# Adding a unit's two key blocks into one square before the transpose, and splitting it by two masks after

## The chip, the core and the metric

The kernel runs on one core of one Trainium2 chip. The metric is the device time of one execution in microseconds (us); lower is better. The engines are named as the profile names them: PE (TensorE matmul) and PEld (its weight load), DVE (VectorE), ACT (ScalarE), POOL (GpSimd) and SP (SyncE, whose queue issues the DMAs).

## What is computed

Attention with four sink keys and a sliding window of 128, for 4 batches of 8 heads, 768 positions and 64 dimensions per head, followed by a feed-forward layer on the 3072 x 512 result:

```python
scores = scale * np.matmul(q, k.transpose(0, 1, 3, 2))
rel = pos[:, None] - pos[None, :]
keep = (pos[None, :] < n_sink) | ((rel >= 0) & (rel < window))
scores = np.where(keep, scores, -1000000000.0)
a = np.exp(scores - scores.max(-1, keepdims=True))
x = (a / (a.sum(-1, keepdims=True) + 1e-09)) @ v      # heads side by side: 3072 x 512
r = np.maximum(x @ w_in, 0.0)                         # 3072 x 2048
out = (s * (r * r) + b) @ w_out                       # 3072 x 512
```

Everything is float32. The kernel keeps that precision on PE by splitting each operand into a rounded high part and a remainder (hi and lo), and by adding two or three products of the parts.

## The kernel before

**Chunks and steps.** The 3072 rows are eight chunks of 384 (half a batch each). The feed-forward layer of chunk c runs while the attention of chunk c+1 is computed, in one interleaved program (lines 672 to 682). A chunk's feed-forward is 32 steps: for each of 16 blocks f of the inner dimension, l1(f) is 12 matmuls of 384 columns into `h` (L521), followed by L524 and L528 on ACT and L526 and L529 on DVE, which make `g`; l2(f), which stands two blocks later, is 9 matmuls of 512 columns into `po` (L540). Between the steps stand the slots of the next chunk's attention. The attention of chunk 0 has a form of its own (`first_slots`), and the feed-forward of chunk 0 carries, beside the attention of chunk 1, the preparation of the weights: per block f, ACT L198 and L199, DVE L200 and L201, POOL L203, ACT L208, and L214 on DVE or, for every fourth block, on POOL. The last chunk's feed-forward has no attention beside it.

**Units.** One attention unit is a head h and a block i of 128 queries; a chunk has 24 units, and unit t starts in slot t. `unit_a` makes the scores with two matmuls (L293, L294) into `sc`; DVE L298 adds the mask and takes the row minimum of the negated scores; ACT L304 takes the exponential into `sm`; POOL L305 copies the sink columns into `psk`. A unit's `sm` holds two key blocks of 128 columns, the block before the query block (at column p0) and the query block's own (at c0), and 16 sink columns. Since the window is 128, the mask leaves in the earlier block only keys above the diagonal and in the own block only keys on or below it: of a query's 256 entries, position j of one block or position j of the other is zero. Chunks of odd number start in the middle of a batch, and all 24 of their units have two blocks; in chunks of even number the 8 units with i = 0 have no earlier block (g = 0, p0 is None) and 16 have two.

**From exponentials to output.** `unit_b`, LB = 2 slots after `unit_a`, transposes both blocks on PE (L316 for the earlier block, L317 for the own one) into the PSUM tile `tp`; ACT L321 writes the rounded part of `tp` to `hl`, DVE L322 the remainder. `unit_c`, LC = 4 slots after `unit_a`, multiplies `hl` by the values (L354), copies with ACT L362 and adds with DVE L363 into `xm`, and at the end of a pair of heads transposes `psk` (L367) and makes `xsk` of it (ACT L369, DVE L370). `unit_d`, one slot later (LD), has two matmuls (L378, L380), DVE L381 and L382, ACT L383 and POOL L384, which write the pair's part of the next feed-forward's input. `prep_head` splits a head's queries (ACT L268, DVE L272), keys (ACT L271, POOL L273) and values (ACT L277, POOL L278); `load_sinks` has ACT L259 and POOL L260.

**What sets the order.** The program is written as the loops above; a list scheduler of the kernel language puts the instructions of each engine in order when the kernel is built, and each engine then works through its own list in that order. Tiles come from pools of buffers: a write into a buffer waits until the readers of what it held are done. `sm` has four buffers, `hl` two, `xm` two, and all tiles named by `ps` (`sc`, `tp`, `h`, `o`, `ts`, `os`, `zb`) share five banks of PSUM.

Of the kernel before, what the change touches and what calls it, by code (L numbers as in the profile page):

```python
# [6 lines left out]
F32 = mybir.dt.float32  # L7
# [5 lines left out]
ALU = mybir.AluOpType  # L13
AX = mybir.AxisListType

P = 128
# [3 lines left out]
CH = BLK * P  # L20
# [6 lines left out]
MDT = mybir.dt.bfloat16  # L27
# [6 lines left out]
E0, LB0, LC0 = 8, 4, 6  # L34
LB, LC, LD, L2 = 2, 4, 1, 2


@with_exitstack
def tile_kernel(ctx, tc, qT, kT, k0, v, vsk, n_sink, window, w, s, b, out):
    nc = tc.nc  # L40
    w, n_sink, window = (a.bitcast(I32) for a in (w, n_sink, window))
    const = ctx.enter_context(tc.tile_pool(name="const", bufs=1))
# [7 lines left out]
    wk = wk_cm.__enter__()  # L50
# [8 lines left out]
    ident = identr.bitcast(F32)  # L59
# [4 lines left out]
    W = 2 * P + NS  # L64
    msk = const.tile([P, 3 * W + P + NS], MDT, tag="msk", name="msk")
    m_1, m_odd, m_even = (msk[:, j * W:(j + 1) * W] for j in range(3))
    m_0 = msk[:, 3 * W:]
# [29 lines left out]
    def mask(out, keep):  # L97
        nc.vector.tensor_scalar(out=out, in0=keep, scalar1=BIG, scalar2=-BIG, op0=ALU.mult, op1=ALU.add)
# [31 lines left out]
    def constants2():  # L130
# [16 lines left out]
        mask(m_1[:, 2 * P:], tm2[:, :NS])  # L147
        mask(m_even[:, P:P + NS], snk[:, :NS])
        cp = nc.gpsimd.tensor_copy
        upm, lom = m_full[2][:, P:2 * P], m_full[2][:, 2 * P:]  # L150
# [130 lines left out]
    def unit_a(k, h, i):  # L281

        hd = k.heads[h]
# [5 lines left out]
        else:  # L289
# [13 lines left out]
        hh = h % 2  # L303
        nc.scalar.activation(sm[:, :n], sm[:, :n], AF.Exp, bias=negm[:, uu], scale=-1.0, accum_out=pp.zz[:, i, hh:hh + 1])  # L304
        nc.gpsimd.tensor_copy(out=pp.psk[:, i, :6 * NS].rearrange("p (t x) -> p t x", t=3)[:, :, hh * NS:(hh + 1) * NS],  # L305
                              in_=sm[:, s0:s0 + NS].unsqueeze(1).to_broadcast([P, 3, NS]))

    def unit_b(k, h, i):
# [5 lines left out]
        tp = ps("tp")  # L314
        if p0 is not None:
            nc.tensor.transpose(tp[:, :P], sm[:, p0:p0 + P], ident)  # L316
        nc.tensor.transpose(tp[:, P:2 * P], sm[:, c0:c0 + P], ident)  # L317

        a, z = (P if p0 is None else 0), 2 * P
        hi, lo = (hd.hl[:, t, i * z + a:(i + 1) * z] for t in range(2))  # L320
        nc.scalar.copy(hi, tp[:, a:z])  # L321
        nc.vector.tensor_tensor(out=lo, in0=tp[:, a:z], in1=hi.bitcast(F32), op=ALU.subtract)  # L322
        pp = k.pairs[h // 2]
# [9 lines left out]
    def unit_c(k, h, i):  # L333
# [23 lines left out]
        if i == BLK - 1:  # L357
            a, c = (0, D) if h % 2 == 0 else (D, 0)
            if h % 2 == 0:
                pp.x = wk.tile([P, CH], F32, tag="xm", name="xm")  # L360
                pp.y = wk.tile([P, CH], F32, tag="y", name="y", bufs=1)
# [385 lines left out]
```

## Time and profile before

| | us |
|---|---|
| median of 3 timed runs | 783.27 |
| lowest and highest of them | 783.14, 783.36 |
| span of the profiled execution, first to last instruction | 782.6 |
| PE busy in it | 735.8 |
| DVE busy | 510.5 |
| ACT busy | 494.6 |
| POOL busy | 263.8 |

For the profiled execution only its span is recorded, with no total of its own; the span is 0.67 us below the median of the timed runs, and that remainder is taken to lie around it. The page and the views of the trace name a group of instructions by line, engine and operation, then by output and inputs (out<-in), then by shapes and count; the number after the bar is the busy time of the group in us and the mean of one in ns, then the idle time of the engine in front of them and what ended it. A row of the timeline gives start and duration in us. A row of the stretches (windows) gives the stretch, its length, and for each engine the busy time and the count of instructions, then the granted PE clock as a share of full speed, the DMA share and GB/s.

### The profile page before, as it was taken

How to read it: one execution, taken by the hardware profiler on the slowest of the kernel's cores; microseconds unless marked ns; L12 is line 12 of the kernel's file. 1: busy time of each engine (PE TensorE's matmuls, PEld its weight loads, DVE VectorE, ACT ScalarE, POOL GpSimd, SP SyncE). 2: the span in 40 equal slices, each digit the busy share in tenths (PEclk: the TensorE clock that was granted, in tenths of full speed). 3: DMA queues.
4: the chain of work that ended last, by engine and by line, in shares of the span. 5: the costliest groups of instructions: out<-in, count | busy, mean ns of one | idle time of the engine just before them, and what ended most of it. 6: DMA issues, size and time to landing. Idle time of an engine off the chain costs nothing.

```text
span 782.6 us, 12152 instructions
## 1 busy us (share of the span) xinstructions
PE 735.8 (94%) x4036; PEld 656.8 (84%) x4036; DVE 510.5 (65%) x1251; ACT 494.6 (63%) x1231; POOL 263.8 (34%) x411
## 2 busy tenths in 40 slices
PE   6878887599999999999999999999999999999996
PEld 3657675489989999999989999899989999899985
DVE  5888899985676466665676466765676466663231
ACT  4896977766676576656676576656676576643222
POOL 3146567752333234332333234322333234210000
PEclk9998999989999999999999999999999999999999
DMA  8644304212111211112111211112111211001001
GB/s 275 267 148 176 111 14 160 85 34 75 43 44 53 85 46 52 49 43 76 43 43 54 85 46 52 50 43 76 43 44 55 83 46 54 27 1 41 1 1 44
DMA packets 28118, 54.21 MB, mean 69 GB/s; under 512 B 3600, under 2 KB 16528, under 8 KB 26128
## 3 DMA queue, kind: packets, MB, share of 16 engines
q1 hardware_dynamic: 28048, 53.36, 21.3%
q8 instruction: 34, 0.56, 0.3%
q14 instruction: 36, 0.29, 0.1%
HBM read 47.06 MB, written 6.29 MB: 68 GB/s over the span
## 4 chain that ended last, share of the span: by engine, by line
PE 77%; DVE 7%; ACT 6%; POOL 4%; issue 3%; DMA 1%; SPq 1%; ACTq 0%; POOLq 0%; DVEq 0%
PE h L521 31%; PE po L540 30%; PE o L354 5%; PE sc L294 2%; PE sc L293 2%; POOL w L203 2%; PE tp L317 2%; PE tp L316 2%; DVE w L201 1%; ACT w L199 1%; DVE wt L200 1%; PE o L480 1%; DMA sb<-in_s 1%; ACT sm L304 1%; ACT w L208 1%
## 5 line engine op out<-in xcount | busy, mean ns | idle before, releaser
L521 PE MATMUL h<-x,w 128*128 128x384 f32 x1536 | 300.9, 345 | 14.3 <-DVE r L526 8.1
L540 PE MATMUL po<-w,g 128*128 128x512 f32 x1152 | 298.5, 401 | 4.3 <-DVE g L529 3.2
L521 PEld LDWEIGHTS h<-x,w 128*128 128x128 f32 x1536 | 270.5, 190 | 22.0 <-issue 5.9
L540 PEld LDWEIGHTS po<-w,g 128*128 128x128 f32 x1152 | 209.7, 189 | 45.7 <-DVE g L529 5.0
L524 ACT ACTIVATE r<-h 128x384 f32<-128x384 f32 x128 | 62.7, 490 | 109.4 <-PE h L521 102.3
L298 DVE CUSTOM_DVE_ANT_0 sm<-sc,msk 128x272 f32<-128x272 f32 (+1 forms) x168 | 70.2, 418 | 82.0 <-PE sc L294 60.2
L529 DVE SCALAR_TENSOR_TENSOR g<-r,sb,g 128x384 fp32r<-128x384 f32 x128 | 86.6, 677 | 45.1 <-ACT g L528 43.0
L526 DVE SCALAR_TENSOR_TENSOR r<-h,sb,r 128x384 f32<-128x384 f32 x128 | 78.5, 614 | 54.3 <-ACT r L524 54.1
L305 POOL COPY psk<-sm 128x48 f32<-128x48 f32 x168 | 51.8, 309 | 168.2 <-ACT sm L304 167.3
L304 ACT ACTIVATE sm<-sm,negm 128x272 f32<-128x272 f32 (+1 forms) x168 | 85.3, 508 | 22.9 <-DVE negm L298 22.0
L528 ACT ACTIVATE g<-r,sb 128x384 fp32r<-128x384 f32 x128 | 78.8, 615 | 29.3 <-DVE r L526 29.1
L273 POOL TENSOR_TENSOR kl<-kraw,kh 128x544 fp32r<-128x544 f32 (+1 forms) x56 | 71.8, 1282 | 56.4 <-ACT kh L271 54.5
L321 ACT CAST hl<-tp 128x256 fp32r<-128x256 f32 (+1 forms) x168 | 59.0, 352 | 27.5 <-PE tp L317 27.1
L354 PE MATMUL o<-hl,vv 128*128 128x256 f32 (+1 forms) x400 | 71.6, 295 | 1.8 <-DVE hl L322 0.9
L322 DVE TENSOR_TENSOR hl<-tp,hl 128x256 fp32r<-128x256 f32 (+1 forms) x168 | 66.6, 398 | 7.9 <-ACT hl L321 6.0
L278 POOL TENSOR_TENSOR vv<-vraw,vv 128x256 fp32r<-128x256 f32 (+1 forms) x56 | 42.9, 766 | 60.8 <-ACT vv L277 58.7
L354 PEld LDWEIGHTS o<-hl,vv 128*128 128x128 f32 x400 | 55.0, 190 | 4.1 <-issue 1.3
L363 DVE TENSOR_TENSOR xm<-o,y 64x384 f32<-64x384 f32 x56 | 31.0, 553 | 31.5 <-ACT y L362 31.3
L294 PE MATMUL sc<-kl,qs 128*128 128x272 f32 (+1 forms) x168 | 48.8, 290 | 0.4 <-POOL kl L273 0.4
L293 PE MATMUL sc<-kh,qs 128*128 128x272 f32 (+1 forms) x168 | 47.8, 284 | 0.7 <-DVE qs L272 0.4
L272 DVE TENSOR_TENSOR qs<-qraw,qs 64x384 fp32r<-64x384 f32 x56 | 42.5, 758 | 6.3 <-ACT qs L268 4.6
L317 PE MATMUL tp<-identr,sm 128*128 128x128 f32 x168 | 46.0, 274 | 0.0
(113 smaller groups left out, 838.7 us busy)
## 6 DMA issues: line engine op xcount, KB each, us to landing
w<-in_w SPq DMA_DIRECT2D x15, 1024.0 KB, 10.3
kraw<-in_kT SPq DMA_DIRECT2D x32, 272.0 KB, 2.6
out<-ot SPq DMA_DIRECT2D x24, 256.0 KB, 2.0
qraw<-in_qT SPq DMA_DIRECT2D x28, 192.0 KB, 2.4
kraw<-in_kT SPq DMA_DIRECT2D x24, 208.0 KB, 2.4
vraw<-in_v SPq DMA_DIRECT2D x16, 256.0 KB, 2.6
vraw<-in_v SPq DMA_DIRECT2D x12, 192.0 KB, 2.3
vsraw<-in_vsk SPq DMA_DIRECT2D x28, 64.0 KB, 1.8
```

The lines of the kernel that those rows point to most:

```text
L273: nc.gpsimd.tensor_tensor(out=hd.kl[:, :kw], in0=hd.k[:, :kw], in1=hd.kh[:, :kw].bitcast(F32), op=ALU.subtract)
L293: nc.tensor.matmul(sc[:, :n], hd.qs[:, qs], hd.kh[:, c0:c0 + n], start=True, stop=False)
L294: nc.tensor.matmul(sc[:, :n], hd.qs[:, qs], hd.kl[:, c0:c0 + n], start=False, stop=True)
L298: nc.vector.tensor_tensor_reduce(out=sm[:, :n], in0=sc[:, :n], in1=m, scale=-0.125, scalar=BIG, op0=ALU.add, op1=ALU.min, accum_out=negm[: ...
L304: nc.scalar.activation(sm[:, :n], sm[:, :n], AF.Exp, bias=negm[:, uu], scale=-1.0, accum_out=pp.zz[:, i, hh:hh + 1])
L322: nc.vector.tensor_tensor(out=lo, in0=tp[:, a:z], in1=hi.bitcast(F32), op=ALU.subtract)
L354: nc.tensor.matmul(hd.o[:, q0:q0 + n * P], hd.vv[:, kb, :], hd.hl[:, t, c0 * P:(c0 + n) * P], start=(hd.n == 0), stop=(i == BLK - 1 and kb ...
L521: nc.tensor.matmul(h[:, :CH], weight[f][:, 0, wi, cc * P:(cc + 1) * P], x[xi][:, cc, :], start=(i == 0), stop=(i == 11))
L526: nc.vector.scalar_tensor_tensor(out=r, in0=h[:, :CH], scalar=sw_ap, in1=r, op0=ALU.mult, op1=ALU.mult)
L528: nc.scalar.activation(gg[:, 0, :], r, AF.Identity, bias=b_ap, scale=1.0)
L529: nc.vector.scalar_tensor_tensor(out=gg[:, 1, :], in0=r, scalar=b_ap, in1=gg[:, 0, :].bitcast(F32), op0=ALU.add, op1=ALU.subtract)
L540: nc.tensor.matmul(po[tb], gg[:, gi, tsl], weight[f][:, 1, wi, :], start=(f == 0 and i == 0), stop=(f == NF - 1 and i == 2))
```

## The change

Units with two key blocks (144 of the 168 that `unit_a` and `unit_b` work on) get another path. Behind the exponential, POOL adds the earlier block of `sm` onto the own block (after.py L311, 128 x 128, both inputs and the output in SBUF), ahead of the copy of the sinks. `unit_b` transposes this one square (L322). DVE multiplies the transposed square, read twice from PSUM, by `split`, two masks of ones and zeros held as bf16, into a new SBUF tile `two` with one buffer (L332); ACT rounds `two` into `hl` (L334), and POOL instead of DVE takes the remainder (L335). The 24 units without an earlier block keep their one transpose, ACT copy and DVE remainder. Two small DVE instructions make `split`, once. `unit_b` comes three slots after `unit_a` (LB) instead of two and `unit_c` five (LC) instead of four, so that the distance from `unit_b` to `unit_c` stays at two slots; `xm` has one buffer instead of two.

```diff
--- before.py
+++ after.py
@@ -32,7 +32,7 @@
 NARROW, NEARLY = 2, 8
 RB, VB = 2, 2
 E0, LB0, LC0 = 8, 4, 6
-LB, LC, LD, L2 = 2, 4, 1, 2
+LB, LC, LD, L2 = 3, 5, 1, 2
 
 
 @with_exitstack
@@ -63,6 +63,7 @@
     n_ap, w_ap = nw[:, 0:1], nw[:, 1:2]
     W = 2 * P + NS
     msk = const.tile([P, 3 * W + P + NS], MDT, tag="msk", name="msk")
+    split = const.tile([P, 2, P], MDT, tag="split", name="split")
     m_1, m_odd, m_even = (msk[:, j * W:(j + 1) * W] for j in range(3))
     m_0 = msk[:, 3 * W:]
 
@@ -146,6 +147,8 @@
         mask(m_0[:, :NS], tmp[:, :NS])
         mask(m_1[:, 2 * P:], tm2[:, :NS])
         mask(m_even[:, P:P + NS], snk[:, :NS])
+        nc.vector.tensor_scalar(out=split[:, 0, :], in0=rel, scalar1=0.0, scalar2=None, op0=ALU.is_gt)
+        nc.vector.tensor_scalar(out=split[:, 1, :], in0=rel, scalar1=0.0, scalar2=None, op0=ALU.is_le)
         cp = nc.gpsimd.tensor_copy
         upm, lom = m_full[2][:, P:2 * P], m_full[2][:, 2 * P:]
         cp(out=m_0[:, NS:], in_=lom)
@@ -302,6 +305,10 @@
         s0 = k.cc[(h, i)][3]
         hh = h % 2
         nc.scalar.activation(sm[:, :n], sm[:, :n], AF.Exp, bias=negm[:, uu], scale=-1.0, accum_out=pp.zz[:, i, hh:hh + 1])
+        if g > 0:
+            c1 = k.cc[(h, i)][1]
+            p1 = k.cc[(h, i)][2]
+            nc.gpsimd.tensor_tensor(out=sm[:, c1:c1 + P], in0=sm[:, p1:p1 + P], in1=sm[:, c1:c1 + P], op=ALU.add)
         nc.gpsimd.tensor_copy(out=pp.psk[:, i, :6 * NS].rearrange("p (t x) -> p t x", t=3)[:, :, hh * NS:(hh + 1) * NS],
                               in_=sm[:, s0:s0 + NS].unsqueeze(1).to_broadcast([P, 3, NS]))
 
@@ -312,14 +319,20 @@
         if i == 0:
             hd.hl = wk.tile([P, 2, 2 * CH], F32R, name="hl", tag="hl", bufs=HLB)
         tp = ps("tp")
-        if p0 is not None:
-            nc.tensor.transpose(tp[:, :P], sm[:, p0:p0 + P], ident)
-        nc.tensor.transpose(tp[:, P:2 * P], sm[:, c0:c0 + P], ident)
-
-        a, z = (P if p0 is None else 0), 2 * P
-        hi, lo = (hd.hl[:, t, i * z + a:(i + 1) * z] for t in range(2))
-        nc.scalar.copy(hi, tp[:, a:z])
-        nc.vector.tensor_tensor(out=lo, in0=tp[:, a:z], in1=hi.bitcast(F32), op=ALU.subtract)
+        nc.tensor.transpose(tp[:, :P], sm[:, c0:c0 + P], ident)
+
+        z = 2 * P
+        if p0 is None:
+            hi, lo = (hd.hl[:, t, i * z + P:(i + 1) * z] for t in range(2))
+            nc.scalar.copy(hi, tp[:, :P])
+            nc.vector.tensor_tensor(out=lo, in0=tp[:, :P], in1=hi.bitcast(F32), op=ALU.subtract)
+        else:
+            hi, lo = (hd.hl[:, t, i * z:(i + 1) * z] for t in range(2))
+            two = wk.tile([P, 2, P], F32, tag="two", name="two", bufs=1)
+            nc.vector.tensor_tensor(out=two, in0=tp[:, :P].unsqueeze(1).to_broadcast([P, 2, P]), in1=split, op=ALU.mult)
+            flat = two.rearrange("p s c -> p (s c)")
+            nc.scalar.copy(hi, flat)
+            nc.gpsimd.tensor_tensor(out=lo, in0=flat, in1=hi.bitcast(F32), op=ALU.subtract)
         pp = k.pairs[h // 2]
         if h % 2 == 1 and i == BLK - 1:
             zr = wk.tile([P, 2, BLK, 2], F32, tag="zr", name="zr")
@@ -357,7 +370,7 @@
         if i == BLK - 1:
             a, c = (0, D) if h % 2 == 0 else (D, 0)
             if h % 2 == 0:
-                pp.x = wk.tile([P, CH], F32, tag="xm", name="xm")
+                pp.x = wk.tile([P, CH], F32, tag="xm", name="xm", bufs=1)
                 pp.y = wk.tile([P, CH], F32, tag="y", name="y", bufs=1)
             nc.scalar.copy(pp.y[a:a + D], hd.o[c:c + D, :CH])
             nc.vector.tensor_tensor(out=pp.x[a:a + D], in0=hd.o[a:a + D, :CH], in1=pp.y[a:a + D], op=ALU.add)
```

PE, in the middle of the attention of a chunk with an odd number: before, from the scores of one unit to the last product of the next, with one l2 step (`po`) between them.

```order
L293 MATMUL sc<-kh,qs 128x272
L294 MATMUL sc<-kl,qs 128x272
L316 MATMUL tp<-identr,sm 128x128
L317 MATMUL tp<-identr,sm 128x128
L354 MATMUL o<-hl,vv 128x256 x2
L354 MATMUL o<-hl,vv 128x128 x2
L540 MATMUL po<-w_792,g 128x512 x9
L293 MATMUL sc<-kh,qs 128x272
L294 MATMUL sc<-kl,qs 128x272
L316 MATMUL tp<-identr,sm 128x128
L317 MATMUL tp<-identr,sm 128x128
L354 MATMUL o<-hl,vv 128x128 x2
```

A place of the same kind in the changed kernel, two l2 steps further on (L296 and L297 are the scores, L322 the transpose, L367 the products with the values, L553 the l2 step).

```order
L296 MATMUL sc<-kh,qs 128x272
L297 MATMUL sc<-kl,qs 128x272
L322 MATMUL tp<-identr,sm 128x128
L367 MATMUL o<-hl,vv 128x256 x2
L367 MATMUL o<-hl,vv 128x128 x2
L553 MATMUL po<-w_971,g 128x512 x9
L296 MATMUL sc<-kh,qs 128x272
L297 MATMUL sc<-kl,qs 128x272
L322 MATMUL tp<-identr,sm 128x128
L367 MATMUL o<-hl,vv 128x128 x2
L367 MATMUL o<-hl,vv 128x256 x2
```

Each unit has one transpose fewer on PE; the scores, the products and the feed-forward steps stand as they stood.

POOL, in the feed-forward of chunk 0 while the weights are made: before, a stretch with two of the weight steps (L203); `vv` and `kl` are the splits of values and keys, `psk` the copy of the sinks.

```order
L278 TENSOR_TENSOR vv<-vraw,vv 128x4x64
L305 COPY psk_96<-sm 128x3x16
L305 COPY psk_95<-sm 128x3x16
L203 TENSOR_TENSOR w_801<-w_801 128x1024
L273 TENSOR_TENSOR kl<-kraw,kh 128x544
L305 COPY psk_95<-sm 128x3x16
L203 TENSOR_TENSOR w_896<-w_896 128x1024
```

The changed kernel, from one weight step (L206) to the next (`sm` is the new addition, `hl` the new remainder).

```order
L206 TENSOR_TENSOR w_802<-w_802 128x1024
L281 TENSOR_TENSOR vv<-vraw,vv 128x4x64
L311 TENSOR_TENSOR sm<-sm 128x128
L312 COPY psk_96<-sm 128x3x16
L335 TENSOR_TENSOR hl<-two,hl 128x256
L311 TENSOR_TENSOR sm<-sm 128x128
L312 COPY psk_96<-sm 128x3x16
L335 TENSOR_TENSOR hl<-two,hl 128x256
L311 TENSOR_TENSOR sm<-sm 128x128
L312 COPY psk_96<-sm 128x3x16
L335 TENSOR_TENSOR hl<-two,hl 128x256
L206 TENSOR_TENSOR w_900<-w_900 128x1024
```

Where one or two copies of sinks stood between two weight steps, three additions, three copies and three remainders now stand between these two.

## The prediction

> **What bounds the kernel now.** First the page: its engine line, and two rows of the span in 40 slices.
>
> ```profile
> PE 735.8 (94%) x4036; PEld 656.8 (84%) x4036; DVE 510.5 (65%) x1251; ACT 494.6 (63%) x1231; POOL 263.8 (34%) x411
> ...
> PE   6878887599999999999999999999999999999996
> DVE  5888899985676466665676466765676466663231
> ```
>
> PE is at 9 in every slice but the first eight and the last, and there DVE is the fuller engine. So one answer does not hold for the whole span, and I cut it into stretches: the feed-forward of chunk 0 with the making of the weights, a short run-out of it, the six chunks after it, and the last feed-forward alone.
>
> ```profile
> 56.00:164.00 108.00, 84.90 (x409) 68.96 (x408) 99.11 (x164) 82.75 (x167) 69.95 (x62) 0.92 0.31 106
> 164.00:182.50 18.50, 17.12 (x96) 15.15 (x96) 11.91 (x26) 10.81 (x26) 9.47 (x12) 1.00 0.23 74
> 182.50:708.00 525.50, 523.06 (x3013) 482.34 (x3012) 338.43 (x890) 339.47 (x899) 167.36 (x308) 1.00 0.18 51
> 708.00:782.60 74.60, 67.42 (x338) 60.55 (x336) 19.94 (x33) 20.15 (x37) 0.63 (x1) 0.98 0.06 23
> ```
>
> In the six chunks PE is busy 523.06 of 525.50 us (99.5%) at the full granted clock, with DVE and ACT at 64 to 65% and POOL at 32%. In the first stretch no engine is full: DVE 92%, PE 79%, ACT 77%, POOL 65%. The views of the waits say how they hold each other there, and that PE in the six chunks hardly waits at all (its only row):
>
> ```profile
> PE os L378 <- DVE xsk L370: 2.4, 6, 0.5
> ...
> ACT w L208 <- POOL w L203: 14.2, 10, 2.1
> PE h L521 <- DVE r L526: 8.1, 4, 5.5
> ```
>
> So in the six chunks the end is set by what PE has to do, and in the first stretch by a ring of DVE, ACT and POOL.
>
> **What goes from PE.** The changed part has one transpose where L316 and L317 stood. A busy time doesn't price it, since matmuls overlap; the starts do. One unit, with nothing but an l2 step behind it:
>
> ```profile
> 307.38 0.29 PE L293 MATMUL sc<-kh,qs 128*128 128x272 f32 x1
> 307.50 0.29 PE L294 MATMUL sc<-kl,qs 128*128 128x272 f32 x1
> 307.63 0.27 PE L316 MATMUL tp<-identr,sm 128*128 128x128 f32 x1
> 307.74 0.27 PE L317 MATMUL tp<-identr,sm 128*128 128x128 f32 x1
> 307.77 2.35 PE L540 MATMUL po<-w,g 128*128 128x512 f32 x9
> ```
>
> Four matmuls take 0.39 us of the stream (0.10 each), and L317 starts 0.11 after L316, L316 0.13 after L294. The chain of waits over the six chunks gives the same for all of them, with the count of L316 in that stretch in the second row:
>
> ```profile
> by line: PE h L521 38.3%; PE po L540 36.1%; PE o L354 6.7%; PE sc L294 3.1%; PE sc L293 3.0%; PE tp L317 2.7%; PE tp L316 2.3%; PE ts L367 1.1%; PE os L378 1.1%; PE zb L380 0.8%; ACT g L528 0.7%; DVE xsk L370 0.6%; DVE xm L363 0.6%; issue 0
> ...
> 182.50:708.00 525.50, 32.90 (x120) 16.74 (x120) 1.00 0.18 51
> ```
>
> L316 is 2.3% of 525.5 us, 12.1 us for 120, or 0.101 each. Bounds: 0.10 to 0.13, 12.1 to 15.6 us. I take 0.105, near the chain's, so 120 x 0.105 = **12.6 us less** in the six chunks. The other 24 removed transposes lie in chunk 1's attention, in the first two stretches, where PE has room; they count for nothing there, at best 24 x 0.105 = 2.5 us.
>
> The Trainium skill, TensorE: Matmul & The Clock Gate, section Back-to-back issue gap, puts a sustained stream of pairs of weight load and matmul at 128 columns at about 81 ns per matmul; an estimate by that would be 120 x 0.081 = 9.7 us. The same page's section on LDWEIGHTS gives columns divided by 1.2 ns, 107 ns for 128. The trace's 101 to 110 ns speaks for the second.
>
> **What comes to POOL, ACT and DVE.** POOL gets 128 x 128 additions and 128 x 256 remainders with all operands in SBUF. Nearest rows in the six chunks, with the DVE remainder that goes:
>
> ```profile
> L260 POOL TENSOR_TENSOR vs<-vsraw,vs 32x128 fp32r<-32x128 f32 x24 | 10.9, 455 | 53.6 <-issue 39.7 <-ACT vs L259 13.6
> L278 POOL TENSOR_TENSOR vv<-vraw,vv 128x256 fp32r<-128x256 f32 x24 | 18.1, 754 | 22.7 <-ACT vv L277 21.1
> L273 POOL TENSOR_TENSOR kl<-kraw,kh 128x544 fp32r<-128x544 f32 x24 | 32.6, 1357 | 29.2 <-ACT kh L271 28.0 <-PE tp L317 1.2
> L305 POOL COPY psk<-sm 128x48 f32<-128x48 f32 x144 | 38.9, 270 | 161.1 <-ACT sm L304 160.3
> ...
> L529 DVE SCALAR_TENSOR_TENSOR g<-r,sb,g 128x384 fp32r<-128x384 f32 x96 | 59.6, 621 | 31.0 <-ACT g L528 29.2
> L322 DVE TENSOR_TENSOR hl<-tp,hl 128x256 fp32r<-128x256 f32 x120 | 50.1, 417 | 7.6 <-ACT hl L321 6.0
> L272 DVE TENSOR_TENSOR qs<-qraw,qs 64x384 fp32r<-64x384 f32 x46 | 29.0, 631 | 5.1 <-ACT qs L268 3.6
> ...
> L321 ACT CAST hl<-tp 128x256 fp32r<-128x256 f32 x120 | 44.2, 369 | 26.8 <-PE tp L317 26.5
> L277 ACT CAST vv<-vraw 128x256 fp32r<-128x256 f32 x24 | 9.4, 393 | 0.0
> ```
>
> Per unit POOL gets 0.455 + 0.754 = 1.21 us. The mask multiplication on DVE has the operands' places of L322 (one from PSUM, one from SBUF, 256 columns), so I price it at the 417 ns that L322 takes away: zero net. ACT's rounding reads SBUF instead of PSUM: 393 against 369 ns, 24 x 120 = 2.9 us of an engine that is 65% busy, hidden. The two instructions that make `split` and the copy of the smaller g = 0 tile are below a microsecond and not in the six chunks.
>
> In the six chunks POOL rises by 120 x 1.21 = 145 us to 313 of some 513, 61%: room. What must hold is the time from transpose to product. Before, in one unit:
>
> ```profile
> 301.66 0.27 PE L317 MATMUL tp<-identr,sm 128*128 128x128 f32 x1
> ...
> 303.15 0.35 ACT L321 CAST hl<-tp 128x256 fp32r<-128x256 f32 x1
> ...
> 303.53 0.42 DVE L322 TENSOR_TENSOR hl<-tp,hl 128x256 fp32r<-128x256 f32 x1
> ```
>
> The remainder is ready 2.3 us after the transpose starts, and is read two slots later; a chunk is 525.5 / 6 = 87.6 us for 29 slots, so a slot is 3.0 us and two are 6.0. In the changed kernel the multiplication stands where DVE waited anyway, and the remainder takes 0.754 instead of 0.42: 2.6 us. In front of it on POOL stand the next unit's addition and copy (0.455 + 0.270) and, at worst, `kl` and `vv` together (1.36 + 0.75): 5.4 us, still within 6.0. The new wait is on DVE: with one `two`, a multiplication waits for POOL's remainder of the unit before, and L526, L529 and the next L298 queue behind it. With 5.4 us against a slot of 3.0 that will happen in slots with a `kl`; DVE's third of idle time covers about 1 us per slot of it, and `g` is read two blocks later. If that cover were gone, `h` would hold its bank longer and PE would stall (priced below). The addition stands in front of POOL's sink copy, and the transpose waits for it; the extra slot of LB covers its 0.455. `xm` with one buffer is written two slots after POOL L384 of the pair before has read it, 6.0 us for a chain of some 3: nothing. The third slot's delay at the chunk's end costs nothing, as slot 30 of 30 falls behind the same step as slot 29 of 29 did.
>
> **What it costs in the first stretch.** There the wait for POOL is on the path, and one more thing shows: DVE instructions whose operands are both in SBUF stretch while POOL works.
>
> ```profile
> 102.26 2.20 POOL L203 TENSOR_TENSOR w<-w 128x1024 int32<-128x1024 int32 x1 [1.16 <-DVE w L201]
> 102.74 2.13 DVE L272 TENSOR_TENSOR qs<-qraw,qs 64x384 fp32r<-64x384 f32 x1
> ...
> 302.88 0.55 DVE L272 TENSOR_TENSOR qs<-qraw,qs 64x384 fp32r<-64x384 f32 x1
> ...
> L529 DVE SCALAR_TENSOR_TENSOR g<-r,sb,g 128x384 fp32r<-128x384 f32 x13 | 14.1, 1086 | 1.0 <-ACT g L528 0.7
> L272 DVE TENSOR_TENSOR qs<-qraw,qs 64x384 fp32r<-64x384 f32 x6 | 9.5, 1579 | 0.2
> L203 POOL TENSOR_TENSOR w<-w 128x1024 int32<-128x1024 int32 (+1 forms) x14 | 26.7, 1913 | 9.6 <-DVE w L201 7.6 <-ACT w L199 2.0
> ```
>
> L272 took 2.13 us beside an L203, 0.55 beside nothing. In the first stretch L529 and L272 have 13 x (1086 - 621) + 6 x (1579 - 631) ns = 11.7 us more than at the means of the six chunks, at a POOL share of 65% against 32%: 35 us per unit of share. The 21 units of this stretch add 21 x 1.21 = 25.4 us to POOL's 69.95: 88%, and by that slope 0.23 x 35 = 8 us to DVE, which is idle for 8.9. So the stretch grows by somewhere between 0 (all in idle time) and 8 us; I take **5 us more**.
>
> **The sum.** 782.6 - 12.6 + 5 = 775.0 of span, and with the 0.67 us around it 775.7 in the timed runs.
>
> **Rivals.**
> - *The first stretch takes the gain back* (slower). POOL's remainder waits for ACT, which waits for DVE, which waits for `two`; L203 stands behind it in POOL's list, and L208 behind L203 on ACT. For it: the 14.2 us that ACT already waits for L203, DVE at 92%. Against: POOL still has 38 us idle there. Price: the 8 us of DVE plus a remainder of 0.754 in front of each of 13 L203, 9.8: about 18; 783.3 - 12.6 + 18 = 788.7. It decides from the point where the stretch grows by more than 12.6 us. The Trainium skill, SBUF — State Buffer, section Terms, has a rule for this: VectorE and GpSimd share a port pair that one instruction locks for its whole length while the other fully blocks; the row of L272 at 2.13 us agrees. 0.18.
> - *PE waits for late remainders in the six chunks* (no change). The margin of 0.6 us goes if DVE's or ACT's queue adds 0.75 us; then the products of each of the 48 heads start 0.15 us late, 7.2 us in all: 783.3 - 12.6 + 5 + 7.2 = 782.9. Against it: 2.4 us of waits in 525.5. 0.12.
> - *The first stretch doesn't feel it* (faster still). The third slot of LB loosens the ring, POOL's work falls into its idle time, and PE's 24 transposes count too: 783.3 - 12.6 - 2.5 = 768.2. 0.17.
> - That the transposes do not go is ruled out by the rows of the order shown with the change.
>
> **Chances and range.** The forecast has 0.53; with growth of 0 to 8 us and 12.1 to 15.6 us saved, its own range is 767.7 to 779.2. The range reaches from a little below the forecast's own lower end, with the third rival's 768.2 inside it, to a microsecond past the second's 782.9: 767.5 to 784.0. It leaves out the first rival, 0.18. About 0.2% (1.6 us) is what a measurement of this kernel can tell from no change. Faster by more: 0.53 + 0.17 and a little of the second, 0.73; the same 0.10; slower 0.17, nearly all the first rival.
>
> **What would show it.** Right: 168 transposes in all instead of 312, the stretch of the six chunks shorter by 12 to 13 us with PE still above 99%, POOL near 60% in it, additions near 0.46 and remainders near 0.75 us, multiplications near 0.42; the first stretch 3 to 8 us longer, with DVE's L529 and L272 stretched more. Wrong: PE waiting for `hl` in the six chunks, a first stretch longer by over 12 us, or a chain in which the six chunks shrink by less than 0.08 us for each transpose.

## The result, and the profile after

The changed kernel takes **788.70 us** (median of 4 runs, 787.42 to 789.21) against 783.20 for the kernel before: a ratio of 1.006, 95% interval 1.0046 to 1.0073, so it is slower by about 5.5 us. The forecast was 775.7, faster, with a range to 784.0. It was wrong.

The profiled execution of the changed kernel has a time of its own, 789.21 us, for a span of 787.4: 1.8 us lie around the span. Every execution of this study that has both numbers shows 1.7 to 2.3; the 0.67 us taken for the kernel before, a span beside the median of other executions, is too small by about a microsecond, which the forecast's 775.7 carries with it. In the page's engine line, POOL went from 34% to 57%, and PE has 144 instructions fewer than the 4036 of before. The slices of PE show a 9 from the eleventh to the last but one; before, it was from the ninth.

```profile
PE 728.6 (93%) x3892; PEld 644.0 (82%) x3892; DVE 535.6 (68%) x1253; ACT 498.8 (63%) x1231; POOL 447.2 (57%) x699
...
PE   6877777778999999999999999999999999999996
```

To cut both spans at the same work I use one mark: the start of the `os` matmul that ends a pair of heads. Chunk 1's attention has four of them, and the last of the kernel is the 28th. Here are the fourth and the 28th before,

```profile
177.62 0.34 PE L378 MATMUL os<-xsk,vs 128*128 128x384 f32 x1
...
705.29 0.34 PE L378 MATMUL os<-xsk,vs 128*128 128x384 f32 x1
```

and after:

```profile
190.96 0.34 PE L391 MATMUL os<-xsk,vs 128*128 128x384 f32 x1
...
709.92 0.34 PE L391 MATMUL os<-xsk,vs 128*128 128x384 f32 x1
```

Up to the fourth the changed kernel is 13.3 us later (forecast: 5). From there to the 28th, the six chunks, it takes 518.96 instead of 527.67 us, 8.7 less (forecast: 12.6). Behind the 28th, 77.5 against 77.3. So 13.3 - 8.7 + 0.2 = 4.8 us of span: both terms missed, in the same direction. The first and the third stretch, cut at the same distance from the marks as those of before:

```profile
56.00:177.30 121.30, 89.30 (x415) 71.90 (x415) 99.00 (x174) 87.27 (x173) 103.42 (x109) 0.92 0.28 94
...
195.80:712.60 516.80, 513.03 (x2893) 468.51 (x2893) 366.64 (x890) 340.93 (x899) 315.75 (x548) 1.00 0.17 52
```

In the six chunks PE is still busy 99.3% of the time, and POOL 61%, as forecast. In the first stretch, 13.3 us longer, POOL has 33 us more than before, and DVE no more than it had: 99.0 us, now 82% of the stretch where it was 92%. The granted clock of this stretch is 0.92 in both. In the 13.7 us between its end and the mark it is 0.75, where it was 1.00; PE is busy in 10.5 of them, so by an estimate from these numbers the lower clock accounts for a quarter of that, 2.6 us, at most. Whether it is lower because PE waited more is not shown.

**The six chunks.** The new instructions take about what they were priced at. From the groups of the six chunks:

```profile
L335 POOL TENSOR_TENSOR hl<-two,hl 128x256 fp32r<-128x256 f32 x120 | 101.1, 842 | 12.0 <-ACT hl L334 11.2
...
L311 POOL TENSOR_TENSOR sm<-sm 128x128 f32<-128x128 f32 x120 | 59.5, 496 | 94.0 <-ACT sm L307 92.4
...
L332 DVE TENSOR_TENSOR two<-tp,split 128x256 f32<-128x256 f32 x120 | 50.1, 418 | 5.5 <-POOL hl L335 3.3 <-PE tp L322 1.0
```

The transpose also saves what it should. The unit with only an l2 step behind it, which took 0.39 us of PE's stream, now takes 319.53 - 319.25 = 0.28:

```profile
319.25 0.29 PE L296 MATMUL sc<-kh,qs 128*128 128x272 f32 x1
...
319.53 2.35 PE L553 MATMUL po<-w,g 128*128 128x512 f32 x9
```

What is missing went into a wait. Before, PE's weight load waited for `xsk` in six of the 24 units with `os` and `zb`,

```profile
PEld os L378 <- DVE xsk L370: 3.9, 6, 0.7
```

and after, in 18:

```profile
PEld os L391 <- DVE xsk L383: 9.3, 18, 0.9
```

The same unit in both kernels shows where that comes from. The rows are starts and durations; first PE, ACT and DVE of before,

```profile
337.00 0.29 PE L293 MATMUL sc<-kh,qs 128*128 128x272 f32 x1
...
337.39 0.42 PE L378 MATMUL os<-xsk,vs 128*128 128x384 f32 x1
...
337.83 0.40 PE L540 MATMUL po<-w,g 128*128 128x512 f32 x1
...
336.00 0.48 ACT L369 CAST xsk<-ts 128x384 fp32r<-128x384 f32 x1
...
336.60 0.55 DVE L370 TENSOR_TENSOR xsk<-ts,xsk 32x384 fp32r<-32x384 f32 x1
```

then the same engines of after:

```profile
347.73 0.28 PE L296 MATMUL sc<-kh,qs 128*128 128x272 f32 x1
...
347.98 0.27 PE L322 MATMUL tp<-identr,sm 128*128 128x128 f32 x1
348.40 0.44 PE L391 MATMUL os<-xsk,vs 128*128 128x384 f32 x1
...
348.85 0.39 PE L553 MATMUL po<-w,g 128*128 128x512 f32 x1
...
346.27 0.40 ACT L334 CAST hl<-two 128x256 fp32r<-128x256 f32 x1
346.69 0.47 ACT L375 COPY y<-o 64x384 f32<-64x384 f32 x1
347.19 0.48 ACT L382 CAST xsk<-ts 128x384 fp32r<-128x384 f32 x1
...
347.79 0.55 DVE L383 TENSOR_TENSOR xsk<-ts,xsk 32x384 fp32r<-32x384 f32 x1
```

Before, `xsk` was finished at 337.15, ahead of `os`. After, ACT's copy of `y` and its `xsk` stand behind the rounding L334, so `xsk` is finished at 348.34, and `os` starts at 348.40, although the one transpose started at 347.98. The unit takes 1.12 us where it took 0.83. The rounding did not wait here, nor in any of the 18 units: it starts as soon as ACT's work before it ends. In this unit its 0.40 us ahead of the two copies makes most of the difference: ACT's copy of `xsk` starts 0.54 us ahead of the first score matmul, where it was 1.00.

**The first stretch.** The groups of the stretch, for the instructions the forecast spoke of:

```profile
L335 POOL TENSOR_TENSOR hl<-two,hl 128x256 fp32r<-128x256 f32 x21 | 19.6, 934 | 1.6 <-ACT hl L334 1.6
...
L311 POOL TENSOR_TENSOR sm<-sm 128x128 f32<-128x128 f32 x24 | 19.5, 813 | 1.0 <-ACT sm L307 0.8
...
L542 DVE SCALAR_TENSOR_TENSOR g<-r,sb,g 128x384 fp32r<-128x384 f32 x14 | 15.9, 1137 | 1.5 <-ACT g L541 1.4
...
L275 DVE TENSOR_TENSOR qs<-qraw,qs 64x384 fp32r<-64x384 f32 x6 | 5.0, 842 | 0.2
```

DVE's stretching, the mechanism the forecast priced, did not grow in the sum: the `g` instruction has a mean of 1137 ns (1086 before), but the `qs` instruction 842 (1579 before). POOL's additions, 0.45 us alone, have a mean of 813. The waits of the stretch name the new step, on DVE and on ACT:

```profile
DVE two L332 <- POOL hl L335: 16.2, 10, 2.6
ACT w L211 <- POOL w L206: 12.6, 9, 2.8
ACT hl L334 <- DVE two L332: 10.4, 8, 4.0
```

One jam, read from POOL, then DVE, then ACT:

```profile
99.42 3.39 POOL L217 TENSOR_TENSOR w<-w,w 128x1024 fp32r<-128x1024 f32 x1
102.76 2.21 POOL L206 TENSOR_TENSOR w<-w 128x1024 int32<-128x1024 int32 x1
104.94 1.66 POOL L276 TENSOR_TENSOR kl<-kraw,kh 128x544 fp32r<-128x544 f32 x1
106.56 0.45 POOL L311 TENSOR_TENSOR sm<-sm 128x128 f32<-128x128 f32 x1
...
107.13 0.73 POOL L335 TENSOR_TENSOR hl<-two,hl 128x256 fp32r<-128x256 f32 x1
...
107.90 0.42 DVE L332 TENSOR_TENSOR two<-tp,split 128x256 f32<-128x256 f32 x1 [2.51 <-POOL hl L335]
...
108.36 0.40 ACT L334 CAST hl<-two 128x256 fp32r<-128x256 f32 x1 [4.01 <-DVE two L332]
```

A remainder stands behind 7.1 us of the weights' and the keys' work on POOL; the next multiplication waits for it, and ACT for the multiplication. The weights' step stands behind the added work as well. One such place, first DVE, then POOL:

```profile
131.63 1.21 DVE L204 SCALAR_TENSOR_TENSOR w<-w,wt 128x1024 int32<-128x1024 int32 x1
...
133.40 1.44 POOL L311 TENSOR_TENSOR sm<-sm 128x128 f32<-128x128 f32 x1
...
135.30 2.30 POOL L206 TENSOR_TENSOR w<-w 128x1024 int32<-128x1024 int32 x1
```

DVE's part of the weights is ready at 132.84, and POOL's step starts at 135.30, behind a split of values, the addition and its sink copy. Summed over the 16 weight steps up to the mark (the fourth `os`), this delay is 17.0 us, against 7.1 before; additions and remainders fill 6.4 of the 17.0. ACT's wait for POOL's step is not longer than before all the same (12.6 us against 14.2). Whether the wait for `two` is the cause or only the place where the delay shows is what the experiments ask.

### The profile page after: what moved, and what is told of

Read it like the earlier page. It is cut to its first block, busy times and chain, and to the rows that moved or that the text cites. A ratio compares the mean times of both kernels' runs of the same rounds, so it can differ in the third digit from the quotient of the medians.

```text
span 787.4 us, 12241 instructions
## 1 busy us (share of the span) xinstructions
PE 728.6 (93%) x3892; PEld 644.0 (82%) x3892; DVE 535.6 (68%) x1253; ACT 498.8 (63%) x1231; POOL 447.2 (57%) x699
## 4 chain that ended last, share of the span: by engine, by line
PE 67%; DVE 10%; ACT 8%; POOL 7%; issue 5%; DMA 1%; SPq 1%; ACTq 0%; POOLq 0%; DVEq 0%
PE po L553 28%; PE h L534 26%; PE o L367 4%; ACT sm L307 2%; PE sc L297 2%; POOL hl L335 2%; PE sc L296 2%; POOL w L206 2%; DVE xsk L383 1%; PE tp L322 1%; DVE xm L376 1%; PE os L391 1%; DVE w L204 1%; POOL sm L311 1%; POOL kl L276 1%
## 5 line engine op out<-in xcount | busy, mean ns | idle before, releaser
L553 PE MATMUL po<-w,g 128*128 128x512 f32 x1152 | 303.6, 404 | 4.3 <-DVE g L542 2.4
L553 PEld LDWEIGHTS po<-w,g 128*128 128x128 f32 x1152 | 211.4, 191 | 44.8 <-DVE g L542 3.4
L542 DVE SCALAR_TENSOR_TENSOR g<-r,sb,g 128x384 fp32r<-128x384 f32 x128 | 107.8, 842 | 46.2 <-ACT g L541 44.5
L311 POOL TENSOR_TENSOR sm<-sm 128x128 f32<-128x128 f32 x144 | 79.0, 548 | 95.0 <-ACT sm L307 93.2
L335 POOL TENSOR_TENSOR hl<-two,hl 128x256 fp32r<-128x256 f32 x144 | 123.2, 856 | 13.6 <-ACT hl L334 12.7
L301 DVE CUSTOM_DVE_ANT_0 sm<-sc,msk 128x272 f32<-128x272 f32 (+1 forms) x168 | 69.9, 416 | 47.8 <-PE sc L297 34.2
L367 PE MATMUL o<-hl,vv 128*128 128x256 f32 (+1 forms) x400 | 73.6, 299 | 8.7 <-ACT hl L334 3.1
L332 DVE TENSOR_TENSOR two<-tp,split 128x256 f32<-128x256 f32 x144 | 60.2, 418 | 24.6 <-POOL hl L335 22.4
L334 ACT CAST hl<-two 128x256 fp32r<-128x256 f32 x144 | 57.1, 397 | 20.8 <-DVE two L332 20.1
L367 PEld LDWEIGHTS o<-hl,vv 128*128 128x128 f32 x400 | 56.9, 195 | 13.8 <-POOL hl L335 4.5
L312 POOL COPY psk<-sm 128x48 f32<-128x48 f32 x168 | 49.8, 297 | 24.4 <-ACT sm L307 24.4
L281 POOL TENSOR_TENSOR vv<-vraw,vv 128x256 fp32r<-128x256 f32 (+1 forms) x56 | 40.3, 720 | 26.4 <-ACT vv L280 26.4
L297 PE MATMUL sc<-kl,qs 128*128 128x272 f32 (+1 forms) x168 | 48.8, 291 | 4.3 <-POOL kl L276 4.3
L322 PE MATMUL tp<-identr,sm 128*128 128x128 f32 x168 | 46.6, 277 | 6.1 <-DVE two L332 5.0
```

Of the source, the lines that this page charges most:

```text
L297: nc.tensor.matmul(sc[:, :n], hd.qs[:, qs], hd.kl[:, c0:c0 + n], start=False, stop=True)
L301: nc.vector.tensor_tensor_reduce(out=sm[:, :n], in0=sc[:, :n], in1=m, scale=-0.125, scalar=BIG, op0=ALU.add, op1=ALU.min, accum_out=negm[: ...
L311: nc.gpsimd.tensor_tensor(out=sm[:, c1:c1 + P], in0=sm[:, p1:p1 + P], in1=sm[:, c1:c1 + P], op=ALU.add)
L335: nc.gpsimd.tensor_tensor(out=lo, in0=flat, in1=hi.bitcast(F32), op=ALU.subtract)
L367: nc.tensor.matmul(hd.o[:, q0:q0 + n * P], hd.vv[:, kb, :], hd.hl[:, t, c0 * P:(c0 + n) * P], start=(hd.n == 0), stop=(i == BLK - 1 and kb ...
L542: nc.vector.scalar_tensor_tensor(out=gg[:, 1, :], in0=r, scalar=b_ap, in1=gg[:, 0, :].bitcast(F32), op0=ALU.add, op1=ALU.subtract)
```

## The experiments

Four theories of the first stretch are told apart. A: the ring through the one buffer `two`. B: POOL's added work, which stands in front of what others wait for. C: the longer distances LB and LC. D: DVE, the fullest engine of that stretch, is what bounds it. A second question is what the six chunks lost. "The mark" is the fourth `os` of chunk 1 in the profiled execution (177.6 before, 190.96 after), "the six" the time from it to the 28th (527.7 and 519.0). Executions of one kernel spread by 0.5 to 4 us, so the mark is read to a microsecond or two, and the medians, of about 783.2 to 783.8 for the kernel before beside them, decide.

| kernel | median, us | ratio to before (95%) | the mark | the six |
|---|---|---|---|---|
| after, chunk 1 on the old path | 773.49 | 0.9875 (0.9859 to 0.9892) | 174.95 | 519.0 |
| before, longer distances alone | 783.15 | 0.9988 (0.9979 to 0.9997) | 175.1 | 528.6 |
| after, no buffer `two` | 786.41 | 1.0033 (1.0021 to 1.0045) | 190.0 | 518.7 |
| before, both of POOL's instructions, unread | 795.85 | 1.016 (1.0145 to 1.0174) | 188.7 | 528.3 |
| before, the addition alone, unread | 789.11 | 1.0073 (1.006 to 1.0086) | 182.2 | 528.7 |
| after, chunk 1's remainder on DVE | 784.85 | 1.0015 (1.0006 to 1.0024) | 186.7 | 519.2 |
| after, chunk 1's addition and remainder on DVE | 794.72 | 1.0148 (1.0135 to 1.0162) | 196.2 | 519.8 |
| after, no addition in chunk 1 | 785.93 | 1.0023 (1.0014 to 1.0032) | 188.8 | 519.3 |
| after, LD of two slots | 800.01 | 1.0208 (1.0193 to 1.0222) | 195.2 | 526.2 |
| chunk 1 on the old path, 120 transposes put back | 784.07 | 0.9997 (0.9988 to 1.0006) | 175.8 | 529.3 |
| chunk 1 on the old path, `unit_c` ahead of `unit_b` | 769.71 | 0.9821 (0.9807 to 0.9834) | 172.5 | 517.2 |
| after, `unit_c` ahead of `unit_b` | 785.82 | 1.003 (1.0018 to 1.0042) | 188.3 | 517.2 |

**Chunk 1 on the old path.** The change is made for chunks 2 to 7 only.

```diff
-        if g > 0:
+        if g > 0 and k.c != 1:
             c1 = k.cc[(h, i)][1]
...
+        if p0 is not None and k.c == 1:
+            nc.tensor.transpose(tp[:, :P], sm[:, p0:p0 + P], ident)
+            nc.tensor.transpose(tp[:, P:2 * P], sm[:, c0:c0 + P], ident)
```

> The changed kernel, but chunk 1's attention keeps the old path (no addition, two transposes, remainder on DVE); all other chunks have the new one. Theories A and B both put 13.3 us of loss into the feed-forward of chunk 0: the fourth os matmul comes back to 178 us and the time is 788.7 - 13.3 = 775 (773 to 777). Theory C (the longer lags LB and LC cost it, through the order of the weight steps): most of the loss stays, 782 to 788.

773.49 us: 15.2 less than the changed kernel, with the six at 519.0 as there. The whole loss comes from chunk 1's 24 units; the other chunks keep their gain. The single buffer of `xm` costs nothing there: this kernel has it too, and its mark is that of the longer distances alone (below), which has two.

**Longer distances alone** (the kernel before):

```diff
-LB, LC, LD, L2 = 2, 4, 1, 2
+LB, LC, LD, L2 = 3, 5, 1, 2
```

> The kernel before with the longer lags alone (LB 3, LC 5). Theory B (POOL's added work in front of the weight step costs the first stretch): no loss, the feed-forward of chunk 0 as long as before or up to 3 us shorter, as the run with the old path in chunk 1 hints (fourth os at 174.95 against 177.62): 780 to 784. Theory C (the lags): the fourth os late by several us, 788 to 796.

The mark comes 2.5 us earlier and the six 0.9 us later; the median hardly moves. C falls, and the loss of the first stretch against the same distances is 190.96 - 175.11 = 15.9 us, close to the 15.2 of the medians against the run with the old path in chunk 1.

**No buffer `two`.** The multiplication writes into the unit's own `sm`, and `sm` gets a fifth buffer, so that no multiplication waits for the unit before.

```diff
-            two = wk.tile([P, 2, P], F32, tag="two", name="two", bufs=1)
+            two = sm[:, :2 * P].rearrange("p (s c) -> p s c", s=2)
```

> The changed kernel, but the masked product is written over the unit's own sm tile (dead once its square is transposed) instead of into the one buffer named two, and sm has five buffers instead of four: the multiplication of a unit no longer waits for POOL's remainder of the unit before. Same work on every engine. Theory A (the ring through the one buffer: DVE waits 19.0 us for POOL's remainder in the feed-forward of chunk 0, and ACT behind it 12.0): those waits go, the fourth os matmul of chunk 1 comes at 180 to 183 us instead of 190.96, and the time falls by 8 to 11 us, to 778 to 781. Theory B (the load: POOL's 29 us more of work there and the stretched DVE instructions cost it, whatever the buffers): 787 to 789, os at 189 to 191.

2.3 us come back of 15.2. Of DVE's 19.0 us of waits for POOL's remainder 5.7 are left, now at L301, which needs a buffer of `sm` that the remainder still reads. The products (L367), the next that need the remainder, wait longer than in the changed kernel. Up to the mark, from 56 to 190 us:

```profile
ACT w L211 <- POOL w L206: 12.0, 10, 2.8
...
PEld o L367 <- POOL hl L335: 8.7, 7, 3.0
...
DVE sm L301 <- POOL hl L335: 5.7, 3, 2.5
```

A falls as the main cause: 13.3 us of these waits went and 2.3 us of time came back. The wait for `two` was for the most part where the delay showed.

**POOL's load alone.** The kernel before, with an addition of 128 x 128 and a subtraction of 128 x 256 on POOL in each unit with two blocks, into a tile that nobody reads (and one buffer for `xm`).

```diff
+        if g > 0:
+            more = wk.tile([P, 2 * P], F32, tag="more", name="more", bufs=1)
+            nc.gpsimd.tensor_tensor(out=more[:, :P], in0=sm[:, :P], in1=sm[:, P:2 * P], op=ALU.add)
+            nc.gpsimd.tensor_tensor(out=more, in0=sm[:, :2 * P], in1=sm[:, :2 * P], op=ALU.subtract)
```

> The kernel before (two transposes, rounding on ACT from PSUM, remainder on DVE), with POOL's new work added beside it: for every unit with two blocks a 128 x 128 addition and a 128 x 256 subtraction of sm into a tile that nobody reads; xm has one buffer. Output as before. Theory B (load): the feed-forward of chunk 0 grows by 9 to 15 us as in the changed kernel, time 792 to 798. Theory A (ring): POOL's work falls into its idle time there and only some of the stretching of DVE shows, 783 to 788.

The mark is 11.1 us later, though nothing waits for these results. Its first stretch:

```profile
56.00:175.00 119.00, 89.81 (x409) 74.29 (x408) 97.11 (x164) 82.83 (x167) 98.68 (x107) 0.87 0.29 97
```

Its wait for the weights, which was 14.2 us before:

```profile
ACT w L208 <- POOL w L203: 25.7, 11, 4.3
```

The two groups add 16.7 + 15.7 = 32.4 us of POOL work to the stretch:

```profile
L308 POOL TENSOR_TENSOR more<-sm 128x256 f32<-128x256 f32 x22 | 16.7, 757 | 0.1
...
L307 POOL TENSOR_TENSOR more<-sm 128x128 f32<-128x128 f32 x22 | 15.7, 713 | 3.7 <-ACT sm L304 3.4
```

B's forecast came out: 11.1 / 32.4 = 0.34 us of time for each us of work on an engine that was 65% busy. POOL's weight steps start 22.4 us in all behind DVE's part of them, against 7.1 before. DVE's busy time is lower than before (97.1 against 99.1). The granted clock is lower too, 0.87 against 0.92: if PE were on the path all the time, that would be 89.81 x 0.05 / 0.92 = 4.9 us by this estimate, so not all of the 11.1 need be POOL's queue.

**The addition alone** is the same kernel without the subtraction.

> The kernel before with one more POOL instruction in each unit with two blocks, an addition of 128 x 128 into a tile that nobody reads (the output is the reference's), and one buffer for xm. It is the smaller part of the load that moved the end of chunk 1's attention (the fourth os matmul of that chunk) from 177.6 to 188.7 us. Theory B, each microsecond of POOL's added work costs alike: the addition is 0.455 of 0.455 + 0.754 us, so 0.38 of 11.1 is 4.2 us; the fourth os at about 182, the time 786.5 to 788. Rival, POOL has room up to a point and only the last part costs: less than 1.5 us, 783 to 785. The six chunks as before, 528 us, by both.

The mark is 4.6 us later, near the 4.2 of a cost in proportion, with the granted clock of the stretch at 0.91: there is no free room up to a point. The weight steps start 13.6 us in all behind DVE's part. The median is a microsecond above what was expected; the six are 1.0 us longer, which I can't explain.

**Chunk 1's remainder on DVE.**

```diff
-            nc.gpsimd.tensor_tensor(out=lo, in0=flat, in1=hi.bitcast(F32), op=ALU.subtract)
+            e = nc.vector if k.c == 1 else nc.gpsimd
+            e.tensor_tensor(out=lo, in0=flat, in1=hi.bitcast(F32), op=ALU.subtract)
```

> The changed kernel, but in chunk 1 the remainder is taken on DVE instead of POOL: POOL has 24 x 0.755 = 18 us less of the 29 us that it gained beside the weight steps, DVE 24 x 0.42 = 10 us more. Theory B (POOL's queue in front of the weight step): of the 13.3 us lost some 11/29 stay, the fourth os comes at about 183 us and the time is 779 to 783. Theory D (DVE, the fullest engine of that stretch, or its stretching beside POOL): the stretch grows further, 790 to 800.

Only 3.9 us come back, 4.2 at the mark: between the two forecasts, so neither theory has it right. The subtraction costs nearly as much on DVE as on POOL.

**Chunk 1's addition and remainder on DVE** does the same with the addition, so that POOL has no more to do there than before.

> The kernel after, with chunk 1's additions and remainders on DVE instead of POOL, so that POOL has no more to do in the first stretch than in the kernel before. Theory B (POOL's added work alone): the loss goes, the fourth os of chunk 1 at 176 to 179, the time 774 to 777. Theory D (the ring of that stretch is full, and the added work costs on whichever engine it stands, DVE most, being the fullest): no better than with the remainder alone on DVE, which had 186.7, so 186 to 192 and 784 to 790. In between, 180 to 185, says that both hold in part. The six chunks as in the kernel after, 519 us.

196.2: worse than the changed kernel by 5 to 6 us, D's direction and past D's own range. Its first stretch:

```profile
56.00:182.60 126.60, 92.43 (x390) 75.23 (x390) 114.20 (x210) 85.25 (x172) 75.11 (x66) 0.83 0.29 95
```

POOL is back at 75 us and DVE has 114, 90% of a longer stretch. So taking the work off POOL gives nothing back if DVE gets it. That does not make it free on POOL: the load has only gone to the fuller engine. The granted clock of this stretch is lower as well, 0.83, so not each microsecond of the loss need be DVE's.

**No addition in chunk 1**: both blocks are transposed there as before, and the multiplication, the rounding and POOL's remainder stay.

```diff
+            src = tp[:, :P].unsqueeze(1).to_broadcast([P, 2, P])
+            if k.c == 1:
+                src = tp[:, :z].rearrange("p (s c) -> p s c", s=2)
```

> The kernel after, with no additions in chunk 1: there both blocks are transposed as before, and DVE multiplies the two transposed blocks by the masks (which changes no value), ACT rounds, POOL takes the remainder. So chunk 1 keeps the new way from the transpose to hl and POOL's remainder, and loses POOL's addition. The loss of the first stretch against lags alone is 190.96 - 175.11 = 15.9 us. Theory B, each part of POOL's added work costs by its length: the addition alone on the kernel before cost 4.6 us, so the fourth os of chunk 1 comes back to 186 to 187 and the time to 784 to 785. Rival 1, the new way from the transpose to hl is all that costs: 189.5 to 191, 787.5 to 789. Rival 2, POOL's load costs only past a point, which both parts together pass: 176 to 181, 774 to 779. The six chunks 519 us by all.

2.8 us come back by the medians, 2.1 at the mark: between B's value and rival 1's. The addition, worth 4.6 us by itself, is worth less once the rest of the change stands there. The parts don't add up one by one: `two` 2.3, the addition 2.8 and the remainder's place 3.9 make 9.0 of 15.2.

**LD of two slots** was meant to take the six chunks' wait for `xsk` away.

```diff
-LB, LC, LD, L2 = 3, 5, 1, 2
+LB, LC, LD, L2 = 3, 5, 2, 2
```

> The changed kernel with LD 2 instead of 1: the os and zb matmuls come two slots after the sink transposes instead of one. If the six chunks lose 5.4 us (PE's weight load waits 9.3 us for xsk at 18 os matmuls, 3.9 at 6 before) because ACT's copy for xsk now stands behind a rounding that waits for DVE: those waits go, the six chunks take 509 to 514 us instead of 519, and the time is 782 to 785. If PE is slowed there by something else: no change, 787 to 790.

The expectation missed. The wait for `xsk` goes, but PE then waits at `zb` for DVE's instructions that read other tiles of the shared five banks (`sc` and `h`), so for a bank to come free, as I read it, and the six get 7 us longer (the mark comes 4 us later as well; why is open):

```profile
PE zb L393 <- DVE negm L301: 6.5, 6, 1.1
PE zb L393 <- DVE r L539: 6.2, 6, 1.0
```

**120 transposes put back.** The kernel with chunk 1 on the old path, with a second transpose in each unit with two blocks of the six chunks; what it writes is unread.

```diff
+            if p0 is not None:
+                nc.tensor.transpose(tp[:, P:2 * P], sm[:, p0:p0 + P], ident)
             nc.tensor.transpose(tp[:, :P], sm[:, c0:c0 + P], ident)
```

> The run with the old path in chunk 1 (773.49 us), with the second transpose put back in the 120 units of the later chunks, into columns of tp that nobody reads. It measures the price of a transpose by itself. At 0.105 us each the six chunks take 12.6 us more, 531.6, and the time is 786 (785 to 788). If part of the price is hidden (0.07, as the six chunks' 8.7 us less suggest): 782. If the transposes cost nothing that PE would not wait for anyway: 774.

The six are 10.3 us longer, 0.086 for each. With them PE's wait of the weight load for `xsk` falls from 9.3 to 5.1 us: part of what the transposes took was time in which `os` had to wait anyway. 10.3 + 4.2 = 14.5 us, 0.12 each, would be their price without it, so 0.105 to 0.12 gross.

**`unit_c` ahead of `unit_b`**, in the kernel with chunk 1 on the old path: the copies of `y` and `xsk` come ahead of the rounding.

```diff
-                if 0 <= t - LB < n:
-                    unit_b(k, *units[t - LB])
                 if 0 <= t - LC < n:
                     unit_c(k, *units[t - LC])
+                if 0 <= t - LB < n:
+                    unit_b(k, *units[t - LB])
```

> The run with the old path in chunk 1 (773.49 us), and in every slot unit_c ahead of unit_b, so that ACT's copies for y and xsk stand in front of the rounding that waits for DVE's masked product. If the 18 waits of os for xsk (PE's weight load waits 9.3 us) come from ACT's order: they shrink to the 4 us of before, the six chunks take 513 to 515 us instead of 519.0, and the time is 768 to 770. If not: 772 to 775, or later if the remainders now come late for the products.

This is the fastest kernel of the study, 769.71 us, 1.8% below the kernel before. In 18 of the 24 units of the six chunks the wait for `xsk` is gone or nearly so. In six, the first of each chunk, it is still there:

```profile
PEld os L399 <- PE po L561: 6.0, 6, 1.2
PE os L399 <- DVE xsk L391: 4.3, 6, 1.0
PEld os L399 <- DVE xsk L391: 0.2, 1, 0.2
```

The first row names `po`, but PE's own row of the same six names `xsk`, and in each of them the weight load starts 0.11 or 0.12 us after DVE has finished `xsk`: they wait for `xsk`. So the weight load's waits are 6.2 us, down from 9.3 and still 2.3 above the 3.9 of before. The six are 1.8 us shorter, less than expected, and the first stretch 2.5.

**The same order in the changed kernel**, chunk 1 included:

> The kernel after with unit_c written ahead of unit_b in each slot, chunk 1 included. In the kernel with chunk 1 on the old path this order took the os matmuls' waits for xsk from 9.3 to 0.2 us and was worth 3.8 us, 1.8 in the six chunks and 2.4 in the first stretch. Theory B (POOL's added work sets the first stretch, whatever the order of the units' steps): the fourth os of chunk 1 at 187 to 190, the time 784 to 787. Rival (the first stretch is late because xsk and xm stand behind the roundings that wait for the split): the fourth os at 176 to 182, the time 772 to 779. The six chunks about 517 us by both.

2.9 us come back by the medians, 1.8 in the six. The mark, at 188.3, is 2.7 us earlier, about as much as the same order gave with the old path in chunk 1, and stays within theory B's range: the order of the steps doesn't cause the loss of the first stretch.

## Why the prediction was wrong, point by point

- **What bounds the kernel** was read rightly: PE in the six chunks, a ring of DVE, ACT and POOL in the first stretch. The slices alone don't carry it: by the page's digits DVE is the fuller engine in four of the first eight slices and not in the last. The stretches do, with DVE at 92% and PE at 79%.
- **"12.6 us less" in the six chunks** was mis-sized: 8.7. The 0.105 us of a transpose held (0.39 to 0.28 us for a unit). The step that failed is that only `hl` was followed behind the new path. ACT's rounding became later and now stands directly ahead of `y` and `xsk` in ACT's list, and `os` waits for `xsk`: the weight load's wait rose by 9.3 - 3.9 = 5.4 us. The forecast had looked at PE's row of that wait (2.4 us) and not at the weight load's (3.9). With the other order, where the waits are 2.3 us above before, the six are 10.4 us shorter than before, and 10.4 + 2.3 = 12.7, near the forecast's 12.6.
- **POOL at 61%, the durations, no wait of PE for `hl`** in the six chunks: right or nearly. Additions 496 ns, remainders 842 (forecast 0.46 and 0.75), multiplications 418. The second rival, late remainders, is wrong with them.
- **"5 us more" in the first stretch** is the step that turned the sign: 13.3, or 15.9 against the same distances. The forecast made DVE pay, by a slope of its stretching over POOL's share, and priced POOL's own added work at nothing, since POOL had 38 us of idle time. The runs show the opposite. DVE's busy time did not rise (99.0 against 99.1 us), and work on POOL that nobody reads cost 4.6 and 11.1 us, the larger of them 0.34 of its length. Idle time of an engine at 65% was not free room here: its queue made the 16 weight steps late, by 17.0 us in all where it had been 7.1, and the remainder late for the multiplication behind it.
- **POOL's price there** was 21 x 1.21 = 25.4 us; it was 19.6 + 19.5 = 39.1 in the longer stretch, since the added instructions stretched too (below).
- **The first rival** named the place, the sign and, by chance, the time (788.7). Its mechanism was half right: the added work does stand in front of the weights' steps (6.4 us). But ACT's wait for those steps, which it named, did not grow (12.6 against 14.2), the wait for `two` did not decide (2.3 us), and DVE's 8 us of stretching did not come. It also decided from a lower point than stated, since the six gave 8.7.
- **The third rival**, that the longer distance loosens the ring, is true for 2.5 us and no more.
- **Open**: how the 15 us divide between POOL's load and the longer way from the transpose to `hl`, which now passes DVE, ACT and POOL where it passed ACT and DVE. The delay of the weight steps grew by 9.9 us in the changed kernel and by 15.3 in the run with POOL's load alone, which lost less; so something besides that delay costs in the changed kernel. The single parts return 9.0 us, and both added instructions together cost more on DVE than on POOL. The lower granted clock before the mark has an unknown share. That the ring has no engine with room for them fits all runs, and was not shown by one in which such an engine was free.

## What to carry to other kernels

A stretch in which no engine is full, and several wait for each other, must not be priced by adding work into idle time: count a good part of each added microsecond (here a third, on the emptiest engine), or keep the old form in that stretch and change only the stage that is bound by the engine you relieve; here that alone was worth 1.2%. When a step gets one more engine in its chain, follow not only its result but what stands behind it in each queue it passes: the loss in the PE-bound stage came from a copy that has nothing to do with the change. Put the steps whose readers are near ahead of those whose result is read later.

## What the runs showed of the hardware

POOL's additions in the first stretch ranged from 0.45 to 1.88 us (median 0.46). Ten of the 24 took 0.77 us or more; each of the ten overlaps a DVE instruction with both inputs in SBUF and ends 0.31 to 0.33 us after it. One of them, first DVE, then POOL:

```profile
93.39 1.41 DVE L204 SCALAR_TENSOR_TENSOR w<-w,wt 128x1024 int32<-128x1024 int32 x1
...
93.68 1.45 POOL L311 TENSOR_TENSOR sm<-sm 128x128 f32<-128x128 f32 x1
```

DVE's instruction ends at 94.80, and the addition 0.33 us after it, at 95.13, as if it had done nearly all its work behind it. The Trainium skill, SBUF — State Buffer, in its section Terms, says that VectorE and GpSimd share a port pair which one instruction holds for its whole length while the other fully blocks. These rows agree, with POOL as the one that waits; the forecast looked only for DVE as the one.
